# An attention and gated-product block: the reciprocals of the silu in pieces of 72 columns, and a later goal for the scores

## The chip, the cores and the metric

The kernel runs on one core of one Trainium2 chip. The metric is the device time in microseconds of one launch. The engines of a core are TensorE (PE in the profile, PEld for its weight loads), VectorE (DVE), ScalarE (ACT), GpSimd (POOL) and SyncE (SP), which here only issues DMAs. Each engine takes its instructions in the order in which they were written and waits where a semaphore tells it to.

## What is computed

For x of 2048 rows and 576 columns, normalised by row to xn:

```
qkv = xn @ wqkv                      # 32 heads of 18 columns
p   = softmax(q @ k.T * 18**-0.5)    # each head: 2048 x 2048
s   = concat(p @ v) @ wo
h   = (xn @ w_gate) * (xn @ w_up)    # 4608 columns
g   = silu(h @ w_down)
out = x + s * g
```

## The kernel before, in words

All products work on fp32 values that are split into a high and a low part, and add the three products that matter. The program has three stages.

**The start** normalises x, turns it and makes q, k and v, which go to DRAM.

**The main stage** runs the attention and the gated product at the same time. Its parts are:

- Scores "a" (`a_item`, lines 580 to 590): a matmul of 512 columns, 64 for each head, and VectorE's maximum over its row (line 590). They only find the maxima of the softmax.
- Scores "b" (`b_item`, 614 to 622): the same product again, transposed and with the maxima in it, and ScalarE's exponential (622).
- Visits (`visit`, 1021, and `pv_group`, 626): up to 7 blocks of p @ v in one go (line 631), since they use the PE array in another form than all else. VISIT and size (1011 to 1017) set how many. The 512 blocks make 72 visits of 7 and two of 4 at the end.
- The gated product: 72 units (4 chunks of 512 rows by 18 groups of columns). A unit has up and gate matmuls (`gu_op`, 670) and down matmuls (`down_op`, 712), which VectorE adds up in `acc` (`down_end`, 740). The tiles hs, made by ScalarE and GpSimd (685, 686), are the operands of the down matmuls; a turned copy comes by DMA (702).

A matmul of the first, second or fourth kind uses half of the rows of the PE array, so two streams run beside each other, one on each half. No order is written out by hand. A planner in the program (`order`, 1089) plays the engines with prices of its own while it writes the instructions: 0.2335 us for a matmul of 512 columns on one half and 0.1335 us for one of 288 (line 838), 0.859 us for a block of a visit (1031), and durations on VectorE, ScalarE and GpSimd. It gives each score a goal, a time before which the score isn't written while other work is there:

```python
QUICK, LAST, SOONER = 0.75, 0.75, 10.0
...
return QUICK * i if i < N else QUICK * N + pace * (i - N) - SOONER * max(0.0, (i - TOTAL + 31 * N) / (31 * N))
```

N is 64 and TOTAL 2048. The goal of a "b" score is that of the "a" score 88 places later (`b_goal`, 924), and 0.75 us a score once those run out.

**The silu** (`silu`, 752) of one tile of 128 rows and 576 columns takes steps in a list, `later`: an exponential on ScalarE (758), plus one (761) and four reciprocals of 144 columns (765) on VectorE, and a product on GpSimd (768). Twelve tiles go this way in the main stage, four at the end of each of the first three chunks; they are stored to DRAM by GpSimd's queue (775). `small` (995) gives out one step at a time, when the engine of that step is nearly free by the planner's account, at least 6 us after the step before, and 16 us after the product (KINDS and PAUSES, 988 to 991). A later chunk that reuses `acc` must have the tiles behind it first (`ready(sdone, ...)`, 735).

**The end** (1176 to 1262) makes s @ wo (line 1221: 448 matmuls of 288 columns on all rows), and for each of 16 row tiles `give` (1223) multiplies by g and adds x. The silu of the last four row tiles is done here: after each `give`, a number of steps is taken from `later` (line 1261). Before the change these numbers are 1, 1, 3, 3 for four tiles in turn and 4 from tile 12 on. The attention's output of the last heads comes back from DRAM through `fetch_o` (803), is split by `high` and `low` (811 to 822), and is read by the last group of matmuls of the first four row tiles.

Of the kernel before, what the change touches and what calls it, by code (L numbers as in the profile page):

```python
# [40 lines left out]
def kernel(  # L41
# [11 lines left out]
    _, S, D = x.shape  # L53
# [78 lines left out]
    chores, later = [], []  # L132

    def chore(all=True):
        q = (all and chores) or later
        if q:
            f, a = q.pop(0)
            f(*a)
# [431 lines left out]
    with ExitStack() as mid:  # L570
# [149 lines left out]
        def sums(t):  # L720
            k = t // 4 % 2
            if acc[k] is None:
                if k == 0:
                    a = accp.tile([128, 4, D], FT, name="acc")
                    acc[0] = [a[:, s, :] for s in range(4)]
                else:
                    pair = [wpool.tile([128, 2, D], FT, name="acc2", tag="wraw", bufs=2) for _ in range(2)]
                    acc[1] = [a[:, s, :] for a in pair for s in range(2)]
            return acc[k][t % 4]
# [22 lines left out]
        def silu(t, new, end):  # L752

            box = []

            def first():
                box.append(new())
                nc.scalar.activation(box[0], sums(t), AF.Exp, scale=-1.0)

            def second():  # L760
                nc.vector.tensor_scalar(box[0], box[0], 1.0, None, op0=OP.add)

            def inverse(i):
                e = box[0][:, 144 * i:144 * i + 144]
                nc.vector.reciprocal(e, e)

            def last():
                nc.gpsimd.tensor_tensor(box[0], box[0], sums(t), op=OP.mult)
                end(box[0])

            later.extend([(first, ()), (second, ())] + [(inverse, (i,)) for i in range(4)] + [(last, ())])

        def silu_store(t):
            def end(e):
                nc.gpsimd.dma_start(sg[t * 128:(t + 1) * 128, :], e)
                sdone.add(t)

            silu(t, lambda: wpool.tile([128, D], FT, name="sil", tag="draw", bufs=1), end)
# [32 lines left out]
        def high(k, c):  # L811
            if k == 0:
                hi[c] = fin["ep"].tile([128, 5, 512], FR, name="hi", bufs=2)
            nc.scalar.activation(hi[c][:, k, :], lo[k][:, 512 * c:512 * c + 512].bitcast(FT), AF.Copy)

        def low(k, c):
            part = lo[k][:, 512 * c:512 * c + 512]
            if k < 4:
                nc.vector.tensor_tensor(part, part.bitcast(FT), hi[c][:, k, :].bitcast(FT), op=OP.subtract)
            else:  # L820
                nc.vector.tensor_tensor(hi[c][64:128, 4, :], part[64:128].bitcast(FT), hi[c][64:128, 4, :].bitcast(FT),
                                        op=OP.subtract)
# [6 lines left out]
        def fetch(t):  # L829
            rows = slice(t * 128, (t + 1) * 128)  # L830
            if t < 12:
                ready(sdone, t)
                gin[t] = fin["ep"].tile([128, D], FT, name="gin", bufs=7)
                nc.sync.dma_start(gin[t], sg[rows, :])
            xi[t] = fin["ep"].tile([128, D], FT, name="xi", bufs=8)
            nc.sync.dma_start(xi[t], x2[rows, :])
# [78 lines left out]
        na = nb = 0  # L915
        part = len(units) * (2 * 27 * LONG + 4 * 12 * SHORT) + (TOTAL + N + LEAD) * LONG
        span = part + H * NT * (0.859 - 0.04)
        QUICK, LAST, SOONER = 0.75, 0.75, 10.0
        pace = (PACE * span - QUICK * N - LAST * (N + LEAD)) / (TOTAL - N)

        def a_goal(i):
# [51 lines left out]
        def b_next(r=1):  # L973
# [11 lines left out]
            if i % 4 == 3:  # L985
                due.append((h, i // 4, end + 0.03))

        KINDS = {"piece": (("ACT", 0.43), ("POOL", 1.02)), "dpiece": (("ACT", 0.59), ("POOL", 1.43)),
                 "first": (("ACT", 0.59),), "second": (("DVE", 0.37),), "inverse": (("DVE", 0.96),),
                 "last": (("POOL", 1.43),), "high": (("ACT", 0.55),), "low": (("DVE", 0.65),)}  # L990
        PAUSES = {"last": 16.0, "high": 1.5, "low": 1.5}

# [196 lines left out]
    for t in range(12, NT):  # L1189
        def end_silu(e, t=t):  # L1190
            gin[t] = e
            sdone.add(t)

        silu(t, lambda: ep.tile([128, D], FT, name="gl", bufs=4), end_silu)
# [14 lines left out]
    def banks_of(t):  # L1209
        return [bank("ab"[t % 4], 2) if t % 4 < 2 else bank("g", 1, 2 * (t % 4) - 4 + h) for h in range(2)]  # L1210
# [5 lines left out]
    def product(t, h, p, ps):  # L1216
        a, e = p
        c, r = divmod(t, 4)
        w = wov["w"][:, a, :] if a < 8 else wov["w2"][:, a - 8, :]
        o = lo[e - 4][:, t * 128:(t + 1) * 128] if 4 <= e < 8 else hi[c][:, min(e, 4), r * 128:(r + 1) * 128]  # L1220
        nc.tensor.matmul(ps[h][:, 0:HALF], o, w[:, h * HALF:(h + 1) * HALF], start=p == ALL[0], stop=p == ALL[-1])  # L1221

    def give(t, ps, last=False):
        y = ys[:, t % 4, :]
        ready(sdone, t)
        g = gin.pop(t)
        xt = xi.pop(t)
        for h in range(2):
            cs = slice(h * HALF, (h + 1) * HALF)
            nc.vector.tensor_tensor(y[:, cs], ps[h][:, 0:HALF], g[:, cs], op=OP.mult)  # L1230
            if last:
                nc.vector.tensor_tensor(y[:, cs], y[:, cs], xt[:, cs], op=OP.add)
                nc.sync.dma_start(out2[t * 128:(t + 1) * 128, cs], y[:, cs])
            else:
                nc.gpsimd.tensor_tensor(y[:, cs], y[:, cs], xt[:, cs], op=OP.add)
        if not last:
            (nc.gpsimd if t < 10 else nc.sync).dma_start(out2[t * 128:(t + 1) * 128, :], y)
# [9 lines left out]
    for t in range(NT):  # L1247
        if t >= 4:
            ps[t] = banks_of(t)
        for h in range(2):  # L1250
            for p in ORDER[2] if t < 4 else ALL:
                product(t, h, p, ps[t])
        for _ in range((2, 0, 0, 0, 2, 2, 1, 0, 2, 2, 1, 0, 0, 0, 0, 0)[t]):
            if split:
                k, c = split.pop(0)
                high(k, c)
                low(k, c)
        give(t, ps.pop(t), t >= 14)
        if t + 6 < NT and t + 6 not in xi:
            fetch(t + 6)  # L1260
        for _ in range((1, 1, 3, 3)[t % 4] if t < 12 else 4):
            chore()


# [26 lines left out]
```

## Time and profile before

| | us |
|---|---|
| median of three runs | 2593.03 (2589.69 to 2594.57) |
| the profiled execution | 2593.24 |
| its span, first to last instruction | 2591.4 |
| PE busy | 2573.7 |
| DVE busy | 1918.9 |
| ACT busy | 1459.4 |
| POOL busy | 589.2 |

The span is what the trace covers; 1.8 us of the profiled execution's time lie outside it. The granted TensorE clock was 1.00. Lines of the profile name an engine, a line of the kernel, an operation and the tiles that it writes and reads, a count, and durations. A view of windows gives, for a stretch of time, each engine's busy time and, as (x...), how many of its instructions lie in the stretch.

### The profile page before, as it was taken

Reading aid. Unit: us, or ns where it says so; the run is one execution under the profiler, and the core shown is the slowest. Engines: PE = TensorE matmul, PEld = TensorE weight load, DVE = VectorE, ACT = ScalarE, POOL = GpSimd, SP = SyncE. Lnnn points to the kernel's source line nnn. Section 1 sums busy time; section 2 is a strip of 40 time slices with the busy share of each in tenths; the row PEclk is TensorE's granted clock in tenths of the full one; section 3 lists DMA queues with packets and bytes.
Section 4 is the critical chain, followed back from the end, with each engine's and each line's share of the span. In section 5 each row is a group of like instructions: output and inputs, shape, how many; then the busy total and the mean of one; then the engine's idle time right before and its main releaser. Section 6 shows DMA issues by size and latency. Waiting matters only on the chain.

```text
span 2591.4 us, 59097 instructions
## 1 busy us (share of the span) xinstructions
PE 2573.7 (99%) x24360; PEld 2106.9 (81%) x24360; DVE 1918.9 (74%) x3377; ACT 1459.4 (56%) x2688; POOL 589.2 (23%) x659
## 2 busy tenths in 40 slices
PE   8999999999999999999999999999999999999999
PEld 7899877787888888877888888877788888887779
DVE  6208777777778888877788788877788888777527
ACT  5222666666665555655555565655555565555561
POOL 3114444434421111111111111111111211111115
PEclk9999999999999999999999999999999999999999
DMA  7799989888885666665686556655675666665567
GB/s 240 227 277 276 269 225 225 231 214 228 220 200 178 179 180 178 169 181 158 178 193 174 173 163 184 180 159 173 171 195 153 175 183 175 173 177 169 154 181 253
DMA packets 195897, 504.57 MB, mean 195 GB/s; under 512 B 58112, under 2 KB 116352, under 8 KB 156588
## 3 DMA queue, kind: packets, MB, share of 16 engines
q1 hardware_dynamic: 185676, 489.05, 67.8%
q0 software_dynamic: 9952, 11.74, 1.7%
q8 instruction: 192, 3.15, 0.5%
q14 instruction: 77, 0.63, 0.1%
HBM read 312.21 MB, written 107.61 MB: 162 GB/s over the span
## 4 chain that ended last, share of the span: by engine, by line
PE 96%; DMA 1%; DVE 1%; SPq 0%; issue 0%; ACT 0%; POOL 0%; ACTq 0%; POOLq 0%; DVEq 0%
PE pg L670 35%; PE pg L631 17%; PE pg L712 16%; PE pa L588 12%; PE pb L620 9%; PE pg L395 2%; PE pa L341 2%; PE pb L341 2%; PE pg L1221 1%; PE pa L1221 1%; PE pb L1221 1%; DMA hx<-hs 0%; DMA ring<-sqk 0%; DMA xin<-in_A_x_dram 0%; DVE hl L345 0%
## 5 line engine op out<-in xcount | busy, mean ns | idle before, releaser
L590 DVE TENSOR_REDUCE mx<-pa 128x1 f32<-128x512 f32 x2048 | 1361.6, 684 | 159.1 <-PE pa L588 69.7
L622 ACT ACTIVATE pt<-pb 128x512 f32<-128x512 f32 x2048 | 1154.9, 597 | 564.1 <-PE pb L620 458.9
L670 PE MATMUL pg<-xc,wgu 64*128 64x512 f32 x7776 | 1396.7, 392 | 0.0
L670 PEld LDWEIGHTS pg<-xc,wgu 64*128 64x128 f32 x7776 | 1054.9, 186 | 50.4 <-DVE acc L740 0.2
L620 PE MATMUL pb<-pair,ring 56*128 56x512 f32 x2006 | 788.9, 399 | 0.9 <-DMA ring<-sqk 0.9
L588 PE MATMUL pa<-pair,ring 54*128 54x512 f32 x2001 | 784.7, 398 | 0.3 <-DVE mx L590 0.3
L712 PE MATMUL pg<-wd,hs 64*128 64x288 f32 x3408 | 537.2, 292 | 1.2 <-DVE acc L740 1.2
L712 PE MATMUL pg<-wd,hx 64*128 64x288 f32 x3408 | 528.7, 292 | 1.2 <-DMA hx<-hs 1.1
L712 PEld LDWEIGHTS pg<-wd,hs 64*128 64x128 f32 x3408 | 474.1, 186 | 6.0 <-DVE acc L740 1.9
L712 PEld LDWEIGHTS pg<-wd,hx 64*128 64x128 f32 x3408 | 468.0, 185 | 5.7 <-DMA hx<-hs 1.9
L631 PE MATMUL pg<-pt,vt 128*32 128x512 f32 x4096 | 454.8, 594 | 0.0
L686 POOL TENSOR_TENSOR hs<-us,hs 128x512 fp32r<-128x512 f32 x144 | 186.2, 1293 | 1129.8 <-ACT hs L685 1087.9
L588 PEld LDWEIGHTS pa<-pair,ring 54*128 54x128 f32 x2001 | 363.2, 184 | 82.5 <-issue 47.8
L620 PEld LDWEIGHTS pb<-pair,ring 56*128 56x128 f32 x2006 | 364.7, 184 | 12.0 <-ACT us L675 1.5
L631 PEld LDWEIGHTS pg<-pt,vt 128*32 128x32 f32 x4096 | 125.6, 110 | 284.4 <-issue 280.6
L637 DVE TENSOR_TENSOR oc<-oc,pg 128x512 f32<-128x512 f32 x69 | 47.4, 688 | 320.8 <-PE pg L631 320.6
L740 DVE TENSOR_TENSOR acc<-acc,pg 128x288 f32<-128x288 f32 x544 | 233.8, 443 | 27.1 <-PE pg L712 24.2
L685 ACT ACTIVATE hs<-us 128x512 fp32r<-128x512 f32 x144 | 91.0, 632 | 154.3 <-DVE us L682 152.9
L651 POOL DMA_DIRECT2D sot<-oc x124 | 64.1, 523 | 329.7 <-DVE oc L648 327.6
L610 POOL DMA_DIRECT2D pair<-mt x128 | 78.0, 615 | 225.9 <-DVE mt L605 223.8
L635 ACT ACTIVATE oc<-pg 128x512 f32<-128x512 f32 x32 | 19.2, 599 | 189.2 <-PE pg L631 189.2
L191 POOL TENSOR_TENSOR wgu<-wraw,wgu 128x384 fp32r<-128x384 f32 x108 | 108.3, 1015 | 76.0 <-ACT wgu L190 70.9
(130 smaller groups left out, 1376.8 us busy)
## 6 DMA issues: line engine op xcount, KB each, us to landing
wgu<-swg SPq DMA_DIRECT2D x102, 1152.0 KB
hx<-hs SPq DMA_DIRECT2D x142, 512.0 KB
wd<-swd SPq DMA_DIRECT2D x50, 1152.0 KB
swg<-wgu SPq DMA_DIRECT2D x36, 1152.0 KB
pair<-sqk SPq DMA_DIRECT2D x192, 144.0 KB
ring<-sqk SPq DMA_DIRECT2D x384, 72.0 KB
swd<-wd SPq DMA_DIRECT2D x18, 1152.0 KB
sqk<-hl SPq DMA_DIRECT2D x32, 512.0 KB
```

The costliest lines, as they stand in the source:

```text
L191: nc.gpsimd.tensor_tensor(w[:, 9 + b:12 + b, :], raw[:, b:b + 3, :], w[:, b:b + 3, :].bitcast(FT), op=OP.subtract)
L341: nc.tensor.matmul(p, wq[b, a], xcs[c][:, e, :], start=n == 0, stop=n == len(PAIRS) - 1)
L588: nc.tensor.matmul(p, q[rows, t * 128:(t + 1) * 128], k[rows, c * 512:(c + 1) * 512], start=True, stop=True)
L590: nc.vector.tensor_reduce(mx[h][:, t, c:c + 1], p, axis=AX.X, op=OP.max)
L620: nc.tensor.matmul(p, k[rows, t * 128:(t + 1) * 128], q[rows, c * 512:(c + 1) * 512], start=True, stop=True)
L622: nc.scalar.activation(pt[t, c], p, AF.Exp, scale=scale)
L631: nc.tensor.matmul(p[32 * c:32 * c + 32, :], vt[h // 2][:, t, 6 * (h % 2):6 * (h % 2) + 32], pt[t, c], start=t == ts[0], stop=t == ts[-1])
L670: nc.tensor.matmul(ps, gw[n][half[r], a, :], xg[i][half[r], e, :], start=k == 0, stop=k == len(TERMS) - 1)
L685: nc.scalar.activation(hj[:, 0, :], h32, AF.Copy)
L686: nc.gpsimd.tensor_tensor(hj[:, 1, :], h32, hj[:, 0, :].bitcast(FT), op=OP.subtract)
L712: nc.tensor.matmul(ps[:, 0:HALF], (hx if k else hs)[u][half[r], j, a, s * 128:(s + 1) * 128], dw[u][half[r], k, j, e, :], start=n == 0, st ...
L740: nc.vector.tensor_tensor(a, a, ps[:, 0:HALF], op=OP.add)
```

## The change

The reciprocal takes 72 columns instead of 144, so that a tile has 8 of them and its silu 11 steps instead of 7. Each remains a step of its own in `later`. The planner's duration for the step goes from 0.96 to 0.50 us. The numbers of steps taken after each `give` become 1, 2, 5, 5 and 6 from tile 12 on. SOONER goes from 10 to 9, which moves the goal of score i of head 1 and later by (i - 64)/1984 us to a later time: by nothing at first and by 1 us for the last.

```diff
             def inverse(i):
-                e = box[0][:, 144 * i:144 * i + 144]
+                e = box[0][:, 72 * i:72 * i + 72]
                 nc.vector.reciprocal(e, e)
...
-            later.extend([(first, ()), (second, ())] + [(inverse, (i,)) for i in range(4)] + [(last, ())])
+            later.extend([(first, ()), (second, ())] + [(inverse, (i,)) for i in range(8)] + [(last, ())])
...
-        QUICK, LAST, SOONER = 0.75, 0.75, 10.0
+        QUICK, LAST, SOONER = 0.75, 0.75, 9.0
...
-                 "first": (("ACT", 0.59),), "second": (("DVE", 0.37),), "inverse": (("DVE", 0.96),),
+                 "first": (("ACT", 0.59),), "second": (("DVE", 0.37),), "inverse": (("DVE", 0.50),),
...
-        for _ in range((1, 1, 3, 3)[t % 4] if t < 12 else 4):
+        for _ in range((1, 2, 5, 5)[t % 4] if t < 12 else 6):
             chore()
```

## The prediction, made before the result

> **What bounds the kernel now.** I read the page's first part, then the views of single lines for where stages begin and end, then windows, and last the waits.
>
> ```profile
> PE 2573.7 (99%) x24360; PEld 2106.9 (81%) x24360; DVE 1918.9 (74%) x3377; ACT 1459.4 (56%) x2688; POOL 589.2 (23%) x659
> L670 PE MATMUL pg<-xc,wgu 64*128 64x512 f32 x7776 | 1396.7, 392 | 0.0
> L631 PE MATMUL pg<-pt,vt 128*32 128x512 f32 x4096 | 454.8, 594 | 0.0
> L588 PE MATMUL pa<-ring,pair x47: 387/393/499, 197.7 to 246.6; 54*128 54x512 f32 x47
> L1221 PE MATMUL pa<-wos,hi x80: 290/295/398, 2527.2 to 2575.5; 128*128 128x288 f32 x80
> ```
>
> PE is busy for 99% of the span, but its matmuls overlap (a mean of 392 ns each, though two streams write one every 0.2335 us each), so busy time alone proves little. I count work instead. The main stage goes from the first score at 197.7 us to the first matmul of line 1221 at 2527.2: 2329.5 us. Its matmuls, at the planner's prices of the code: 7776 of line 670 and twice 2048 scores are 11872, and as two streams run at once each takes 0.2335/2 = 0.1168 us: 1386.1. Line 712 has 72 units of 96, 6912 at 0.1335/2 = 0.0668: 461.4. Line 631's 4096 at 0.859/8 = 0.1074: 439.8. The sum is 2287.3, so **all idle time of PE in the main stage is about 42 us**. These rows say what lies in it:
>
> ```profile
> 794.00:1018.00 224.00, 224.00 (x2224) 175.10 (x2224) 179.88 (x316) 127.54 (x234) 37.57 (x44) 1.00 0.62 179
> 1018.00:1242.00 224.00, 224.00 (x2211) 183.55 (x2210) 177.46 (x313) 134.71 (x241) 35.85 (x44) 1.00 0.58 165
> 1384.00:1618.00 234.00, 234.00 (x2304) 189.29 (x2302) 194.99 (x337) 139.05 (x253) 38.65 (x45) 1.00 0.61 174
> 1618.00:1852.00 234.00, 233.54 (x2291) 186.15 (x2289) 181.22 (x317) 135.29 (x242) 34.75 (x45) 1.00 0.61 170
> 1979.00:2204.00 225.00, 225.00 (x2226) 184.40 (x2224) 187.50 (x325) 134.58 (x242) 37.63 (x44) 1.00 0.63 175
> 2204.00:2429.00 225.00, 225.00 (x2223) 179.00 (x2223) 175.06 (x305) 128.50 (x234) 33.55 (x40) 1.00 0.58 165
> ```
>
> The columns are the window, its length, and then busy time and count for PE, PEld, DVE, ACT and POOL. The first, third and fifth window are the three stretches in which the reciprocals of the main stage are given out (16 in each); the others, equally long, follow them and have none. In the same two first windows, lines 712 and 631 alone (PE, then PEld):
>
> ```profile
> 794.00:1018.00 224.00, 79.28 (x672) 75.61 (x672) 1.00 0.62 179
> 1018.00:1242.00 224.00, 78.10 (x662) 74.00 (x663) 1.00 0.58 165
> ```
> ```profile
> 794.00:1018.00 224.00, 49.72 (x448) 13.72 (x448) 1.00 0.62 179
> 1018.00:1242.00 224.00, 43.51 (x392) 12.02 (x392) 1.00 0.58 165
> ```
>
> With reciprocals PE did 672 matmuls of line 712, 448 of 631 and 1104 others: 44.9 + 48.1 + 128.9 = 221.9 us of work in 224. Without, 44.2 + 42.1 + 135.1 = 221.4. **The stretch with reciprocals has no more idle time (2.1 us) than the one without (2.6).** In the other two pairs too the window with reciprocals has more matmuls, 2304 to 2291 and 2226 to 2223, by count alone. Nor does the rest hold much: 2.1 to 2.6 us in 224 us with 7 or 8 visits is 0.3 us a visit, so some 22 of the 42 us belong to the 74 visits, whose number doesn't change.
>
> **The change part by part.** *The reciprocals of the main stage.* 48 go, 96 come.
>
> ```profile
> L765 DVE RECIPROCAL sil<-sil x48: 1009/1042/1047, 794.3 to 2203.4; 128x144 f32<-128x144 f32 x48
> L765 DVE RECIPROCAL gl<-gl x16: 992/1034/1053, 2544.6 to 2578.9; 128x144 f32<-128x144 f32 x16
> L646 DVE RECIPROCAL rc<-tp x32: 252/253/255, 367.5 to 2521.6; 128x16 f32<-128x16 f32 x32
> 793.09 1.28 DVE L590 TENSOR_REDUCE mx<-pa 128x1 f32<-128x512 f32 x2
> 794.28 1.04 DVE L765 RECIPROCAL sil<-sil 128x144 f32<-128x144 f32 x1
> 795.24 1.22 DVE L590 TENSOR_REDUCE mx<-pa 128x1 f32<-128x512 f32 x2
> ```
>
> A reciprocal of 144 columns lasts 1.042 us, but the next instruction starts 795.24 - 794.28 = 0.96 us after it, so 0.08 us overlap. No row has 72 columns. From below it holds VectorE for half of 0.96, 0.48 us. From above, the line through 16 columns (0.253) and 144 (1.042) gives 0.253 + 56 x 0.00616 = 0.598 us, less 0.08: 0.52. I take 0.50, between the two near ends. So VectorE's main-stage work goes from 48 x 0.96 = 46.1 us to 96 x 0.50 = 48.0 (46.1 to 49.9): **+1.9 us (0 to +3.8) of an engine that holds 80% in these windows** (179.88 of 224). What hides it is PE's own work; were that cover gone, it would cost those 1.9 us in full.
>
> What a shorter piece could win is time in which a score waits for VectorE. Line 588's weight loads waited:
>
> ```profile
>   DVE mx L590: 6.7, 31
> ...
>   DVE sil L765: 0.8, 1
> ```
>
> Over the whole main stage that is 6.7 us behind another score's maximum and 0.8 us, once, behind a reciprocal itself. A reciprocal may stand behind the maximum that is waited for, so the gain is bounded by 0 and 7.5 us; as the windows show no more idle time with reciprocals than without, I take 0.
>
> The Trainium skill (VectorE: DVE Perf Modes, The TRN2 errata) speaks against the edit: a fixed time is paid once per instruction, so work should be cut into pieces of 512 elements or more. Its 58 cycles at 0.96 GHz would make 64 more instructions cost 3.9 us of VectorE, an estimate. The rows above agree in kind, since 16 columns take 0.253 us.
>
> *Four more steps for each tile.* Steps come at least 6 us apart, 16 after the product: 7 steps are 52 us, and a tile really takes 56 to 59 us (224, 234 and 225 us for four). Eleven steps are 76 us by the rule and about 84 with the same lag, 336 for four tiles. So the product (POOL, 768), the store that GpSimd's queue issues behind it and the end of each pass move later, by up to 112 us.
>
> ```profile
> L768 POOL TENSOR_TENSOR sil<-sil,acc x12: 1407/1431/1445, 826.7 to 2209.1; 128x576 f32<-128x576 f32 x12
> L775 POOL DMA_DIRECT2D sg<-sil x12: 592/604/627, 828.4 to 2210.8; - x12
> ```
>
> The first pass then ends near 1130 and is wanted at about 1384, where chunk 2 begins to overwrite its sums; the last ends near 2321 instead of 2211, and its stored tiles are fetched only once the last visit is written (`prefetch`). The twelve products and stores hold POOL for 2 us each, and POOL is busy for 38 us of 224; they pass no queue with a deadline. Cost 0; were the cover gone, the 22 steps of two tiles would run in one go, some 11 us.
>
> *SOONER.* Late scores move by up to 1 us. What they leave free is filled by units of the gated product, since the planner writes whatever is ready; PE's work is the same. It matters only where that work runs out, at the end of the main stage:
>
> ```profile
> 2515.90 0.50 PE L620 MATMUL pb<-pair,ring 56*128 56x512 f32 x1
> 2516.33 3.64 PE L631 MATMUL pg<-pt,vt 128*32 128x512 f32 x32
> 2519.90 1.06 PE L712 MATMUL pg<-wdl,hs 64*128 64x288 f32 x12
> ...
> 2527.25 1.86 PE L1221 MATMUL pa<-wos,hi 128*128 128x288 f32 x12
> ```
>
> The last score is followed at once by the last visit, and this by the last unit's down matmuls. If the score ends 1 us later, those 7.35 us of down matmuls are there to fill the gap. Bounds are -1 and +1 us; I take 0.
>
> *The end.* 16 reciprocals become 32, +0.6 us of VectorE (0 to +1.3).
>
> ```profile
> 2527.20:2587.00 59.80, 59.76 (x449) 59.48 (x448) 49.15 (x76) 12.26 (x21) 36.33 (x43) 1.00 0.75 266
> ```
>
> PE works without a gap here, and VectorE has over 10 us to spare. The steps taken after tiles 0 to 11 are 24 of 28 before and 39 of 44 now, so the last tile's silu ends after tile 12 in both. In a group, five short pieces hold VectorE for 2.5 us where three long ones held it for 2.9. Cost 0.
>
> **The sum**: 2593.24 (the profiled execution, 0.2 us over the median of the runs) + 0 + 0 + 0 + 0 = **2593.2 us**.
>
> **The rivals.** *First, the waits go.* The short pieces let the maxima through, and the 7.5 us shrink: 2593.2 - 7.5 = 2585.7 at the very best, 2589.5 with half. For it speaks the one wait behind a reciprocal; against it the windows.
>
> *Second, VectorE is the bound and the added time counts.* The sum of the bounds is +0.6 + 1.9 = 2.5 up to 1.3 + 3.8 = 5.1 us: 2595.7 to 2598.3. For it: 80% busy with a queue in order, and PE's weight loads are only 81% busy. The Trainium skill (Perfetto Trace Analysis, Identifying the Most-Contended Engine) calls the weight loads' share, not the matmuls', the measure of how near PE is to its limit, and by it PE would have room. Against it: PE's missing 19% are the visits, where line 631 has 13.72 us of loads in 49.72 of matmuls, and the work count leaves 42 us in 2329.
>
> *Third, slower: the last visit goes behind the down matmuls.* The place is the end of the main stage. The output of the last visit passes VectorE, a store, a load and the splits, and PE has only the down matmuls and the first groups of line 1221 to cover this:
>
> ```profile
> 2533.18 1.90 DVE L819 TENSOR_TENSOR o<-o,hi 128x512 fp32r<-128x512 f32 x3
> ```
> ```profile
> 2535.48 1.59 PE pg L1221 x12
> 2537.06 1.32 PE pa L1221 x10
> ```
>
> The splits end at 2535.1 and the group that reads them starts at 2537.06 in the chain: 2.0 us to spare. If later scores let the last unit overtake the visit, each us beyond 2.0 counts in full, up to 7.35 - 2.0 = 5.4: 2598.6. Against it: the planner makes the visit as soon as its four blocks are ready, and 1 us is less than 2.0.
>
> *Fourth, the change doesn't do what it says*: the planner is so far behind its goals that SOONER moves nothing. The time is again 2593.2.
>
> **How the numbers follow.** The forecast gets 0.71, with a range of its own of 2590.7 to 2596.2: the whole order after the first moved goal is written anew, and the 20 us of idle time that belong to no visit can come out a few us more or less. The first rival gets 0.10, the second 0.09, the third 0.06, the fourth 0.04. A measurement of this kernel can tell about 0.2%, 5.2 us, from no change. Faster than 2587.8 is the better half of the first rival: 0.05. Slower than 2598.2 is the third, a small part of the second and what the new order may add to the forecast: 0.12. The rest, 0.83, is no change. The range is 2589.5 (half of the first rival) to 2597.5 (most of the second).
>
> **What would show it.** Right: 96 reciprocals of 0.56 to 0.60 us in the main stage; the windows as idle with reciprocals as without; last product near 2320; line 1221 starting within 3 us of 2527 and then without a gap. Wrong: line 588's waits for maxima far from 6.7 us; a gap ahead of the matmuls at 2537; a first start of line 1221 over 5 us away, with the idle time in many small gaps.

## The result and the profile after

The changed kernel takes 2599.77 us (median of 11 runs, 2597.31 to 2601.13), the kernel before 2592.22 (11 runs). The ratio is 1.0028, with a 95% interval of 1.0020 to 1.0036: slower by about 7 us, outside the predicted range. The profiled execution took 2599.86 us, with a span of 2598.1; that is 6.7 us more than the 2591.4 of before.

The page's first part, and the lines of the views of single lines that answer to those of before. Of line 1221, the first row has the first start and the second the last:

```profile
PE 2573.9 (99%) x24360; PEld 2109.4 (81%) x24360; DVE 1924.2 (74%) x3441; ACT 1464.1 (56%) x2688; POOL 590.4 (23%) x659
```
```profile
L588 PE MATMUL pa<-ring,pair x47: 388/392/502, 197.2 to 245.9; 54*128 54x512 f32 x47
...
  DVE mx L590: 12.8, 37
...
  DVE sil L765: 0.8, 1
```
```profile
L1221 PE MATMUL pg<-wos,hi x160: 288/295/302, 2533.5 to 2592.2; 128*128 128x288 f32 x160
...
L1221 PE MATMUL pa<-wos,hi x80: 288/294/403, 2530.2 to 2581.0; 128*128 128x288 f32 x80
```

The same row of before, for the last start there:

```profile
L1221 PE MATMUL pg<-wos,hi x160: 288/295/302, 2530.5 to 2586.7; 128*128 128x288 f32 x160
```

PE does the same matmuls in the same busy time, so the loss is idle time, and it lies in three places. The **main stage** goes from 197.2 to 2530.2 us, 2333.0 instead of 2329.5: +3.5. **Line 1221** takes 62.0 us from its first start to its last instead of 59.4 (59.5 by the rounded rows): +2.5. From that last start to the end of the span it is 5.9 instead of 4.7 us: +1.2. With the main stage's start 0.5 us earlier, this is 6.7. The 1.2 us are not a wait for VectorE: in both traces its last instruction ends 1.28 us after the last matmul starts, and what differs is the time from there to the end, with the last store (4.6 instead of 3.4 us). With the main stage's order of before that time is 2.8 to 3.7 us in four traces, with the change's 3.9 to 5.8 in six. So it seems to go with the order; no run shows why.

In the main stage, scores waited 12.8 us for maxima instead of 6.7, and once for a reciprocal, 0.8 us, as before. (These sums take weight loads, 10.4 instead of 6.3 us, and matmuls together, and can count a stretch twice; the prediction took the 6.7 for weight loads alone.) Part of the new wait begins at another line of VectorE. The view by line and shape of line 602, which negates the maxima of a head (before, then after):

```profile
L602 DVE TENSOR_SCALAR mm<-m 128x16 fp32r<-128x16 f32 x32 | 7.5, 236 | 1.1
```
```profile
L602 DVE TENSOR_SCALAR mm<-m 128x16 fp32r<-128x16 f32 x32 | 10.8, 339 | 1.1
```

Its usual length is 0.17 us; two of the 32 lasted over 0.5 us before and six do after. The timeline of the changed kernel shows one of them, first GpSimd, then VectorE, then PE:

```profile
2081.05 1.29 POOL L686 TENSOR_TENSOR hs<-us,hs 128x512 fp32r<-128x512 f32 x1 [16.21 <-ACT hs L685]
```
```profile
2081.20 1.18 DVE L602 TENSOR_SCALAR mm<-m 128x16 fp32r<-128x16 f32 x1
...
2082.76 1.93 DVE L590 TENSOR_REDUCE mx<-pa 128x1 f32<-128x512 f32 x3
```
```profile
2083.46 0.50 PE L588 MATMUL pa<-pair,ring 54*128 54x512 f32 x1 [0.50 <-DVE mx L590]
```

The negation starts while GpSimd makes the low part of hs and ends with it, at 2082.38 against 2082.34. The maxima behind it come 1 us late, and PE waits 0.5 us for one. The Trainium skill (GPSIMD Engine Reference, Specifications) says that GpSimd shares its SBUF interfaces with VectorE and contends with VectorE's instructions in a mode with two ports or with two inputs in SBUF. The trace shows such a wait and gives its price, 1.0 us here; in which mode the negation ran, it doesn't show.

At the end of the main stage, the last visit and the last unit's down matmuls have changed places in part. The timeline of the changed kernel:

```profile
2517.73 0.37 PE L712 MATMUL pg<-wdl,hs 64*128 64x288 f32 x1
...
2521.25 3.64 PE L631 MATMUL pg<-pt,vt 128*32 128x512 f32 x32
2524.82 0.40 PE L712 MATMUL pg<-wdl,hs 64*128 64x288 f32 x1
```

43 of the 96 down matmuls are done ahead of the visit, which starts 4.9 us later than before (2516.33), while line 1221 starts only 3.0 us later. What follows is in the timelines around 2545 us: PE, VectorE and ScalarE of the changed kernel, then VectorE and PE of before.

```profile
2544.90 0.43 PE L1221 MATMUL pg<-wos,hi 128*128 128x288 f32 x2
2546.73 1.04 PE L1221 MATMUL pa<-wos,hi 128*128 128x288 f32 x6 [1.40 <-DVE ys L1230]
```
```profile
2545.40 0.69 DVE L821 TENSOR_TENSOR hi<-o,hi 64x512 fp32r<-64x512 f32 x1 [0.39 <-ACT hi L814]
2546.12 0.82 DVE L1230 TENSOR_TENSOR ys<-pa,gin 128x288 f32<-128x288 f32 x2
```
```profile
2544.74 0.63 ACT L814 ACTIVATE hi<-o 128x512 fp32r<-128x512 f32 x1 [0.45 <-DMA o<-sot]
```
```profile
2540.84 0.69 DVE L821 TENSOR_TENSOR hi<-o,hi 64x512 fp32r<-64x512 f32 x1 [0.59 <-ACT hi L814]
2541.56 0.82 DVE L1230 TENSOR_TENSOR ys<-pa,gin 128x288 f32<-128x288 f32 x2
```
```profile
2541.94 0.43 PE L1221 MATMUL pg<-wos,hi 128*128 128x288 f32 x2
2542.20 0.99 PE L1221 MATMUL pa<-wos,hi 128*128 128x288 f32 x6
```

PE needs the first tile's bank back for the fifth tile. The bank is freed by the first give (line 1230), which stands in VectorE's queue behind a split (821), which waits for ScalarE and this for a load of the attention's output. The loads stand in SyncE's queue behind the store of the last head, so all of this moves with the last visit. Before, the matmul started 0.64 us behind the give, now 0.61 us: this chain had no margin to speak of. The give now starts 4.56 us later, the matmul's turn would have come 2.96 us later, and the difference, 1.60 us, is the gap (1.70 us from start to start, less the usual 0.13).

A second gap, 0.85 us (0.98 from start to start, less the usual 0.13), is near 2564. Here PE waits for another split, behind two short reciprocals:

```profile
2562.13 1.05 DVE L765 RECIPROCAL gl<-gl 128x72 f32<-128x72 f32 x2
2563.21 0.84 DVE L821 TENSOR_TENSOR hi<-o,hi 64x512 fp32r<-64x512 f32 x1
```
```profile
2564.10 1.32 PE L1221 MATMUL pa<-wos,hi 128*128 128x288 f32 x8 [0.70 <-DVE hi L821]
```

These two are not the only suspects. Ten us earlier in the same queue a plus one of the silu (line 761) lasts 2.14 us; the four of the end stage before the change last 0.44 to 1.23. GpSimd is at work at that time:

```profile
2553.46 0.55 POOL L1237 DMA_DIRECT2D out_dram<-ys  x1 [0.30 <-DMA o<-sot]
2554.02 1.57 POOL L1235 TENSOR_TENSOR ys<-ys,xi 128x288 f32<-128x288 f32 x2
```
```profile
2553.78 2.14 DVE L761 TENSOR_SCALAR gl<-gl 128x576 f32<-128x576 f32 x1
```

Its 1.7 us over the usual 0.45 are twice the gap.

The reciprocals themselves:

```profile
L765 DVE RECIPROCAL sil<-sil x96: 559/593/597, 795.4 to 2350.4; 128x72 f32<-128x72 f32 x96
L765 DVE RECIPROCAL gl<-gl x32: 537/545/603, 2548.6 to 2586.0; 128x72 f32<-128x72 f32 x32
```

### The profile page after: what moved, and what is told of

Same layout as the page of the kernel before. It is cut to its first block, busy times and chain, and to the rows that moved or that the text cites. A ratio compares the mean times of both kernels' runs of the same rounds, so it can differ in the third digit from the quotient of the medians.

```text
span 2598.1 us, 59162 instructions
## 1 busy us (share of the span) xinstructions
PE 2573.9 (99%) x24360; PEld 2109.4 (81%) x24360; DVE 1924.2 (74%) x3441; ACT 1464.1 (56%) x2688; POOL 590.4 (23%) x659
## 4 chain that ended last, share of the span: by engine, by line
PE 93%; DMA 3%; DVE 2%; SPq 0%; issue 0%; POOL 0%; ACT 0%; DVEq 0%; ACTq 0%; POOLq 0%
PE pg L670 34%; PE pg L631 17%; PE pg L712 16%; PE pa L588 11%; PE pb L620 9%; PE pg L395 2%; PE pa L341 2%; PE pb L341 2%; PE pg L1221 1%; DMA o<-sot 1%; DMA hx<-hs 0%; DVE mx L590 0%; DMA sg<-sil 0%; DMA wraw<-in_B_w_gate_dram 0%; PE pb L1221 0%
```

## The experiments

Three theories stood at first for the 7 us: the order at the end of the main stage (theory 1), the later goal by itself (theory 2), and the short pieces by themselves (theory 3). "Ratio" is the time against the kernel before in the same set of runs, with its 95% interval.

**SOONER 9 alone** (`e1_goal9`), the kernel before with

```diff
-        QUICK, LAST, SOONER = 0.75, 0.75, 10.0
+        QUICK, LAST, SOONER = 0.75, 0.75, 9.0
```

> The kernel before with SOONER 9 and nothing else. Three theories for the 7 us. Theory 1 (the order at the end of the main stage): only when both edits meet does the planner write 43 of the last unit's 96 down matmuls ahead of the last visit; here it writes none ahead of it, and 38 of the unit before behind it, so the last visit is further from the end of the main stage than before, line 1221 runs without a gap (59.4 us from first to last) and the time is within 3 us of before, 2589 to 2595. Theory 2 (the later goal costs by itself): 2597 to 2601. Theory 3 (the short pieces cost by themselves): 2592, as before, to 1 us.

Measured: 2599.26 us, ratio 1.0028 (1.0017 to 1.0039). Line 1221 hardly has a gap (59.7 us from first to last start) and 134 down matmuls follow the last visit, as theory 1 had it, but the time is as bad as with both edits, since the main stage of the profiled execution takes 2338.2 us, 8.7 more than before (some 1.7 of this is a dip of the clock, see the table below). Theory 1 doesn't explain this one.

**The short pieces alone** (`e2_pieces`), the changed kernel with SOONER 10:

> The changed kernel with SOONER back at 10: the short reciprocals and the new numbers of steps alone. Theory 1 (the order at the end of the main stage): as with SOONER alone, 134 down matmuls follow the last visit, line 1221 has no gap, 2589 to 2596. Theory 2 (the later goal): 2592, as before. Theory 3 (the short pieces): 2597 to 2601, with gaps in line 1221 of 2 to 3 us in sum.

Measured: 2602.41 us, ratio 1.0042 (1.0030 to 1.0055). There is no gap in line 1221 (59.4 us); the main stage takes 2340.9. Each edit alone costs at least as much as both, so they don't add, and none of the three theories had this.

**The end stage as before** (`e3_end_old`), the changed kernel with

```diff
+            w = 72 if t < 12 else 144
...
-                e = box[0][:, 72 * i:72 * i + 72]
+                e = box[0][:, w * i:w * i + w]
...
-[(inverse, (i,)) for i in range(8)]
+[(inverse, (i,)) for i in range(8 if t < 12 else 4)]
...
-(1, 2, 5, 5)[t % 4] if t < 12 else 6
+(1, 1, 3, 3)[t % 4] if t < 12 else 4
```

> The changed kernel, but the four tiles of the silu that are done in the end stage have the 144-column reciprocals and the numbers of steps of before; the main stage is written in the same order as in the changed kernel. Theory 1 (the last visit is late, the short pieces of the end are innocent): the end stage keeps its first gap of 1.5 us near 2545, 2597 to 2600. Theory 3 (the short pieces load VectorE in the end): the end stage gets its 3.7 us back, 2595 to 2596.5.

Measured: 2598.20 us, ratio 1.0025 (1.0015 to 1.0035). The first gap stays (1.68 us near 2544.7), the second goes. The intervals overlap, so the 1.6 us are no more than an indication.

**The end stage as after** (`e4_end_new`), the kernel before with the opposite edit:

> The kernel before with the short reciprocals and the new numbers of steps in the end stage only; the main stage is written in the order of before. Theory 1: no gap in line 1221, since the last visit is as early as before: 2591 to 2593.5. Theory 3: 2595 to 2596.5, with gaps in line 1221 of 2 to 3 us.

Measured: 2593.49 us, ratio 1.0007 (0.9998 to 1.0015), no gap in line 1221. With the old order of the main stage the short pieces cost nothing that can be told. For the end stage theory 3 falls: in these traces the second gap comes only with the late last visit. Here the long plus one is found as well (2.17 us), without a gap behind it. No run has the short pieces of the main stage in the order of before, so what they cost there is known from the waits alone.

**The negation on ScalarE**, in the changed kernel (`e5_neg_act_after`) and in the kernel before (`e6_neg_act_before`):

```diff
-            nc.vector.tensor_scalar(mm[:, 0, :], m, -1.0, None, op0=OP.mult)
+            nc.scalar.activation(mm[:, 0, :], m, AF.Copy, scale=-1.0)
```

> The changed kernel with the small negation of line 602 on ScalarE instead of VectorE; the planner's order is the same. In the changed kernel's trace 6 of the 32 instructions of line 602 last 0.5 to 1.2 us instead of 0.17, all while GpSimd works, in the trace of before 2 do. Theory C (these collisions are most of the main stage's loss): each costs PE about 0.7 us, the main stage ends 2.5 to 3 us sooner and the time is 2596.5 to 2597.5. Rival (a delay of VectorE here is given back by the next pause): 2599 to 2600.5.

> The kernel before with line 602's negation on ScalarE. Theory C: 2 collisions go, 2590 to 2591.5. Rival: the same as before, 2592. If ScalarE itself suffers, slower than 2593.

Measured: 2604.38 us, ratio 1.0050 (1.0037 to 1.0062), and 2601.18, ratio 1.0036 (1.0023 to 1.0048). Both are slower than their parents. The view of line 602 in the second points to the reason:

```profile
L602 ACT ACTIVATE mm<-m x32: 215/216/218, 247.3 to 2443.8; 128x16 fp32r<-128x16 f32 x32
...
  DVE m L596: 37.3, 32
```

ScalarE waits at the negation for VectorE, 1.2 us a head, and the exponentials wait behind it. This says nothing of the held negations; another test of them follows below.

**Two changes of the planner's numbers that do nothing else** asked whether the loss needs the edit at all: SOONER 9.9 (`e7_goal99`), and the price of a reciprocal at 0.97 (`e8_price`):

```diff
-"inverse": (("DVE", 0.96),)
+"inverse": (("DVE", 0.97),)
```

> The kernel before with SOONER 9.9: a goal moved by at most 0.1 us. The planner writes another order from the first heads on. Theory L (any new order loses, since the order of before is an unusually good one and the amounts mean nothing): 2596 to 2602, like SOONER 9. Theory M (the loss grows with the move of the goal): a tenth of what SOONER 9 lost, 2592 to 2593.5.

> The kernel before with the planner's price for a reciprocal at 0.97 instead of 0.96 us; no instruction is added, removed or changed, and the order is that of before until the first reciprocal and another from there on. Theory L: 2595 to 2602 although nothing is done differently. Theory M: 2592, as before, to 1 us.

Measured: 2600.03 us, ratio 1.0032 (1.0020 to 1.0045), and 2603.55, ratio 1.0046 (1.0032 to 1.0059). The second kernel has the instructions of before, and its order up to the first reciprocal, and loses more than the change did. Its main stage, from the views of lines 588 and 1221:

```profile
L588 PE MATMUL pa<-ring,pair x47: 387/392/497, 197.3 to 246.0; 54*128 54x512 f32 x47
```
```profile
L1221 PE MATMUL pa<-wos,hi x80: 288/295/402, 2534.2 to 2585.8; 128*128 128x288 f32 x80
```

2336.9 us, less the 2287.3 of work: 49.6 us idle instead of 42. Not all of this is the order. In this profiled execution the granted clock of PE was at half for 3.41 us near 280 us, which is worth about half of that, 1.7 us, an estimate; the trace of before has no such dip ahead of 2590 us. Two windows of 2 us, `e8_price`, then before:

```profile
279.00:281.00 2.00, 2.00 (x18) 2.00 (x17) 1.33 (x3) 0.61 (x2) 0.00 (x0) 0.50 0.98 339
```
```profile
279.00:281.00 2.00, 1.92 (x26) 1.59 (x24) 2.00 (x4) 1.00 (x3) 0.00 (x0) 1.00 0.99 384
```

The loss itself doesn't hang on it: the two executions of `e8_price` with a mean clock of 1.000 took 2600.9 and 2602.4 us. Theory L takes the place of 1 to 3: another order loses, whatever wrote it.

**The first give ahead of the split** (`e9_give_first`), the changed kernel with

```diff
-        for _ in range((2, 0, 0, 0, 2, 2, 1, 0, 2, 2, 1, 0, 0, 0, 0, 0)[t]):
+        for _ in range((0, 0, 0, 0, 2, 2, 1, 0, 2, 2, 1, 0, 0, 0, 0, 0)[t]):
...
         give(t, ps.pop(t), t >= 14)
+        for _ in range(2 if t == 0 else 0):
+            k, c = split.pop(0)
+            high(k, c)
+            low(k, c)
```

> The changed kernel; only in the end stage, the split of the last two parts of the second 512 columns is written behind the first give instead of ahead of it. Theory E (line 1221's first gap, 1.6 us near 2545, is the give that waits in VectorE's queue behind a split whose data the late last visit holds up): the gap goes or falls under 0.4 us, and the time falls by about 1.3 us, to 2598 to 2599. Rival (the gap is the data of the splits themselves): the gap stays at 1.2 us or more, 2599.5 to 2600.

Measured: 2597.57 us, ratio 1.0022 (1.0013 to 1.0031). The time is a little below theory E's forecast. Both gaps are gone, and line 1221 takes 59.4 us from first to last (59.3 by the rounded rows):

```profile
L1221 PE MATMUL pg<-wos,hi x160: 288/295/302, 2532.4 to 2588.5; 128*128 128x288 f32 x160
L1221 PE MATMUL pa<-wos,hi x80: 288/295/398, 2529.2 to 2577.4; 128*128 128x288 f32 x80
```

**The negation as a reduce**, in the changed kernel (`e10_reduce_after`) and before (`e11_reduce_before`):

```diff
-            nc.vector.tensor_scalar(mm[:, 0, :], m, -1.0, None, op0=OP.mult)
+            nc.vector.tensor_reduce(mm[:, 0, :], m.rearrange("p (t o) -> p t o", o=1), axis=AX.X, op=OP.max, negate=True)
```

> The changed kernel with line 602's negation as a tensor_reduce with negated output, on VectorE and at the same place in its queue, so that ScalarE isn't drawn in as it was in the try before. Theory C (the long instructions of line 602 are held by GpSimd, and a reduce isn't): none of the 32 lasts over 0.5 us, the waits of scores for maxima fall from 12 to about 8 us, the main stage ends 2 to 3 us sooner, 2596.5 to 2598. Rival (held all the same, or given back): 2599 to 2600.5.

> The kernel before with the same negation as a reduce. Theory C: only two long instructions go, 2590 to 2591.5. Rival: 2592, as before, to 0.7 us.

Measured: 2597.18 us, ratio 1.0021 (1.0012 to 1.0029), and 2591.90, ratio 0.9998 (0.9990 to 1.0007). In the changed kernel's trace none of the 32 is long any more:

```profile
L602 DVE TENSOR_REDUCE mm<-m 128x16 fp32r<-128x16 f32 x32 | 5.4, 170 | 1.1
```

So a reduce isn't held by GpSimd where a tensor_scalar is: seven of the 32 start during a tensor_tensor of GpSimd in either trace, and all seven were held before (one for only 0.04 us), none now. But scores still wait 10.5 us for maxima, where theory C had about 8, and the main stage takes 2330.9 us here instead of 2333.0, but in the next two kernels, which have the reduce and the same order, it takes 2333.5 and 2335.1 (2333.4 without a clock dip). That the held negations make the main stage longer is therefore not shown, and most of the delay seems to be given back. In the kernel before there was nothing to win that a measurement shows.

**Three terms together** (`e12_three`): the reduce, the give ahead of the split, and the end stage as in `e3_end_old`.

> The changed kernel with three terms taken away together: the negation as a reduce, the first give ahead of the split, and the end stage's silu with the pieces and steps of before. If the loss is the sum of these terms (2 to 3 us in the main stage, 1.3 and 1.6 in the end): 2593.5 to 2595.5. What then remains over 2592 is spread over the order. If the terms hide one another: 2597 or more.

Measured: 2597.97 us, ratio 1.0020 (1.0011 to 1.0029). They don't add: with the long reciprocals back in the end stage, a gap of 1.0 us appears near 2561. The end from line 1221's last start takes 7.1 us, of which 5.8 lie behind VectorE's last instruction. **The two without the third** (`e13_two_after`):

> The changed kernel with the negation as a reduce and the first give ahead of the split, the end stage's short pieces kept. If the two terms add up (each alone took 2.2 and 2.6 us off the changed kernel's 2599.8): 2594.5 to 2596. If they hide one another, as in the run with three: 2597 to 2598.

Measured: 2595.34 us, ratio 1.0014 (1.0005 to 1.0023), where the first reading expected it. (The profiled execution, 2599.46 us, is the slowest of the eleven.) Line 1221 has no gap again, 59.4 us. **The same two in the kernel before** (`e14_two_before`):

> The kernel before with the same two edits. Its line 1221 had no gap and only two negations were held, so there is little to win: 2590.5 to 2592. If the moved split starts a wait of its own: 2593 or more.

Measured: 2591.86 us, ratio 1.0001 (0.9993 to 1.0010). No version beats the kernel before.

**Two more orders**, the price at 0.95 (`e15_price95`) and SOONER 10.1 (`e16_goal101`):

> The kernel before with the planner's price of a reciprocal at 0.95 instead of 0.96 us, and no other edit. Theory L (the order of before is an unusually good one): 2596 to 2604, like the price 0.97. Rival (0.97 was a bad draw among orders that are mostly as good as that of before): 2590 to 2595.

> The kernel before with SOONER 10.1, earlier scores instead of later ones. Theory L: 2596 to 2604. A theory by which later goals cost and earlier ones win: 2592 or less.

Measured: 2596.66 us, ratio 1.0021 (1.0012 to 1.0030), and 2595.75, ratio 1.0019 (1.0011 to 1.0028). The second is just under theory L's forecast, and clear of 2592. Seven orders other than that of before have now been run with PE's work unchanged; four of them come from a hundredth of a us in a price or a tenth in the goal, of either sign. All seven are slower, by 1.0019 to 1.0046:

| order | ratio | main stage, us | of it a clock dip, us (estimate) | idle in its last part, us | line 1221, us |
|---|---|---|---|---|---|
| before | 1 | 2329.5 | 0 | 4.9 | 59.4 |
| the change | 1.0028 | 2333.0 | 0 | 4.6 | 62.0 |
| SOONER 9 | 1.0028 | 2338.2 | 1.7 | 8.0 | 59.7 |
| short pieces | 1.0042 | 2340.9 | 1.7 | 8.3 | 59.4 |
| SOONER 9.9 | 1.0032 | 2337.6 | 1.7 | 7.0 | 59.4 |
| price 0.97 | 1.0046 | 2336.9 | 1.7 | 8.3 | 62.7 |
| price 0.95 | 1.0021 | 2334.8 | 1.7 | 10.0, with the dip | 59.4 |
| SOONER 10.1 | 1.0019 | 2331.3 | 0 | 7.2 | 60.4 |

All columns but the ratio are of one profiled execution each. In five of them the clock was at half for 3.41 us within the main stage; the table counts half of that. The last part is all from 2200 us behind the first score on, 129 to 141 us; its idle time is its length less the prediction's price of the matmuls that start in it.

How much of a main stage is chance shows where the same order ran again. With that of before (`e4_end_new`, `e11_reduce_before`, `e14_two_before`) it took 2329.0, 2328.5 and 2330.6 us. With that of the change it took 2333.0 and 2332.6 (`e3_end_old`, `e9_give_first`), and 2330.9, 2333.5 and 2335.1 with the reduce, the last with a dip. So 2 to 3 us between two rows say little; the last part's idle time repeats much better, 4.7 to 4.8 us with the order of before and 4.2 to 4.4 with the change's (`e3_end_old`, `e9_give_first`, `e10_reduce_after`, `e12_three`, `e13_two_after`).

That column shows where a part of the loss sits. Six of the seven new orders lose 2 to 3.5 us in the last part of the main stage, where the gated product's units run out, and the seventh, the change, loses 2.5 us in line 1221 instead. With the price at 0.95 and SOONER 10.1 the idle time up to this part is that of before (37.2 and 36.5 us to 37.0), so that all they lose lies from there on. The waits found there are different ones, for example for VectorE's sums of the down products (line 740):

```profile
2522.61 1.66 PE L712 MATMUL pg<-wdl,hs 64*128 64x288 f32 x12 [1.38 <-DVE acc L740]
```

This is of the price 0.95, ahead of the last unit's down matmuls; at the same place PE waits 0.7 us with SOONER 9 and 1.1 with the short pieces alone, and not at all before. No run takes these waits away.

## Why the prediction was wrong, point by point

**What bounds the kernel: right.** PE's work is the bound, and idle time is what moved: 42 us before, 2333.0 - 2287.3 = 45.7 after.

**The reciprocals of the main stage: right, and of no weight.** 72 columns last 0.593 us (forecast 0.56 to 0.60); scores waited 0.8 us once for one, as before. That they cost nothing is read from these waits alone.

**Four more steps a tile: right in sign and cover, the size was off.** The last product of the main stage starts at 2358.7 instead of 2209.1; the forecast of the pass's end was 2321. The prediction took 56 to 59 us for a tile, from windows that leave out the first tile's steps ahead of its reciprocals; from one start of line 761 to the next it was 60 to 77 us, and is 97 to 106 now instead of the forecast 84. In the main stage PE didn't wait for the later products.

**SOONER at 0, with bounds of -1 and +1 us: the step that failed.** The prediction held that a moved goal changes only the end, "since the planner writes whatever is ready; PE's work is the same". PE's work is the same, but a tenth of a us in the goal, or a hundredth in a price, is enough to write another order, and all seven new orders lose 4 to 12 us. The prediction did say that the order would be written anew, and gave this "a few us more or less", as if the order of before were an average one. It is the best of the eight that were run: 4.9 us idle in the last part of the main stage, and no gap in line 1221, though the first give there had no margin left. (Eight are few, and one of eight is the best by chance one time in eight.) The term that the runs show is a one-sided one of +4 to +12 us, and no row of one trace gives it; that the first give came just in time was a hint of its sign.

**The end stage at 0: wrong by 3.7 us**, of which 2.5 are the two gaps; the other 1.2, with the last store, stay without a cause. "VectorE has over 10 us to spare" is a mean over 60 us. What counted was the queue: the first give behind a split, and with the give ahead of it both gaps go in two traces (59.4 us). Whether the second gap comes from the two short reciprocals or from the long plus one ahead of them, no run tells. The third rival had the chain, the last visit partly behind the last unit's down matmuls, but looked for its reader at the matmuls of 2537 with 2.0 us to spare; the reader that ran late is the first give, with none. Its 2598.6, 5.4 us over the forecast, came within 1.2 us of the result by luck: 3.5 of the 7 us lie elsewhere, in the main stage.

**The terms as the runs give them.** By the ratios, the give ahead of the split takes 1.6 us off the changed kernel's loss and the reduce 1.8, and both together 3.6, each with an interval of about 3 us to either side (those of the two ratios combined). Only the two together are clear of noise, and barely. For the give the trace agrees, with 2.6 us less in line 1221; for the reduce it doesn't, since the main stage is no shorter in two of three traces. What remains over the kernel before, ratio 1.0014, has no term of its own. By the trace of the changed kernel it lies in many short waits all along the main stage and in the 1.2 us with the last store; no run takes it away, and why the order of before is better than all others tried stays open.

## What to carry to other kernels

Where a program's order comes from a planner, the forecast of an edit of its numbers has two parts, the edit and a new draw of the order; the second can be larger, and whoever starts from an order that is better than most should expect to lose. Run a change of the planner's numbers that does nothing else before an edit is blamed. For the end of a stage, look at each queue in order for the smallest margin, not at the mean busy share. Before two profiled executions are compared by a few us, look for dips of the clock in each, and see how far the same order differs from itself.

## What the runs showed of the hardware

A tensor_scalar of 128x16 on VectorE, 0.17 us by itself, lasts up to 1.18 us when a tensor_tensor of 1.29 us runs on GpSimd, until that ends: in the changed kernel all seven that started during one were held, the shortest for 0.04 us. A tensor_reduce of the same shape at the same places was held in none of seven. A larger tensor_scalar, of 128x576 (line 761), took 2.14 us instead of 0.45 while GpSimd issued a DMA and ran two tensor_tensors.

The reciprocals kept their length all the while, 0.537 to 0.603 us; 36 of the 128 started while GpSimd was at work.
